# A hand-ordered attention-and-MLP kernel, its instruction order handed to a build-time event model; first loads as token pairs; mask PSUM apart

## Chip, cores, metric

One core of one Trainium2 chip. The metric is the device time of one launch in microseconds (us); lower is better. Names of engines: TensorE (PE in the profile; PEld is its weight load), VectorE (DVE), ScalarE (ACT), GpSimd (POOL), SyncE (SP). SPq, POOLq and ACTq are queues from which transfers are issued.

## The reference

Attention that looks only at the best chunks of keys, then an MLP with a softplus. 4 batches, 8 heads, 768 tokens, head size 64; keys fall into 24 chunks of 32. For each query an upper bound of its score with each chunk is taken from the chunk's minimum and maximum, the 6 chunks with the largest bounds are kept, and softmax runs over those under the causal mask.

```python
k_min, k_max = min and max of k over each chunk of 32 keys
ub = sum over d of max(q * k_min, q * k_max)            # one bound per query and chunk
ub = where(causal, ub, -1e9)
top_chunks = argsort(ub)[..., -6:]
scores = q @ k.T / 8, kept where the chunk is in top_chunks and key <= query
attn = softmax(scores) @ v                               # 4 x 8 x 768 x 64
x = attn, heads side by side                             # 3072 x 512
h = x @ w_in                                             # 512 x 2048
out = softplus(h) @ w_out                                # 2048 x 512
```

## The kernel before

The 3072 tokens are cut into 12 blocks of 256. A block goes through these steps:

1. *prep*: k, q and v are loaded; k and q are turned so that the head size lies on partitions; the chunk extremes `kx`, the bounds `ub` (TensorE), the top 6 (VectorE), and a mask that is turned as well and laid into spare rows of the query tile, so that the score matmul adds it.
2. *scores*: `s_ps` (TensorE), the exponential `pt` (ScalarE), `o_ps` = pt x v (TensorE), division (VectorE), a DMA transpose to `x`.
3. *MLP*: eight groups of eight matmuls `hp` (TensorE), `e_sb` = exp and `g` = ln(1 + e) (ScalarE), then eight groups of four matmuls `y` (TensorE) and the store.

Every engine runs its instructions in the order in which the program lists them. That order was set by hand. Score steps set a slot counter; each slot first runs old work that is due, then some MLP steps by a rate, then whatever an agenda holds for that slot:

```python
def slot(rate):
    cost = 0.0
    for item in list(later):                       # p@v, division, transposes, stores that are due
        if item[0] <= clock[0] and cost < 0.3:
            later.remove(item); cost += item[1]; item[2](*item[3])
    credit[0] += rate
    while credit[0] >= 1.0:                        # MLP steps
        credit[0] -= 1.0
        if next(mlp, "end") == "wait": credit[0] = 0.0
    for g_ in agenda.pop(clock[0], []): next(g_, None)   # prep of later blocks
    ...
    clock[0] += 1

def rate():
    c = clock[0]
    return 0.0 if c < 14 else 1.0 if c < 30 else 0.5 if c < 40 else 1.0 if c < 48 else 0.57 if c < 120 else 1.0
```

The first three blocks are loaded as float32, cast and turned on ScalarE and TensorE, in half blocks; their agenda is a list of numbers (names: c cast, t turn, e evacuate, b extremes, d bounds, `e0` the mask):

```python
stages(f1, ((4, "b0 c0"), (5, "d0"), (6, "ck1 tk1 ek1 cq1 tq1 eq1"), (7, "e0"), (8, "b1 c1"), (9, "d1"), (12, "e1")))
at(11, do(cast_v, 1))
stages(f2, ((18, "ck0 tk0 ck1 ek0"), (19, "b0"), (20, "cq0 tq0 cq1 eq0"), (21, "c0"), (22, "d0"),
            (23, "e0 tk1 ek1"), (24, "b1 tq1 eq1 c1"), (25, "d1"), (27, "e1")))
...
for n in range(3, NB):                             # blocks 3 to 11: loaded as bf16, turned by DMA
    base = 16 * n - 13
    offs = (0, 1, 2, 3, 4, 6, 7, 8, 12)
    turns = (base - 12, max(base - 9, ends[n - 3] + 1))
    if n == 3:
        base, turns = 40, (38, 41)
        offs = (0, 1, 2, 3, 3, 4, 5, 6, 7)
```

The loads of the first blocks take 128 consecutive tokens per transfer, so that one piece is one token of one head, 64 floats or 256 bytes; the mask of a half block uses the one PSUM buffer that the bounds also use:

```python
# load_f32: for t in range(2)
eng[t].dma_start(out=xf[:, t, heads], in_=src[nm][b, heads, r0:r0 + 128].rearrange("h s d -> s h d"))
# prep_first, step e_
mT = ps_t.tile([64, NT, 2, 128], BF16, name="mTh", tag="t")
```

The softmax here doesn't subtract the row's maximum and nothing guards it: scores larger than these inputs give would overflow.

## Time and profile before

| | before |
|---|---|
| time, median of the first 3 runs | 306.91 us (306.29 to 307.59) |
| profiled span | 307.3 us, mean granted TensorE clock 0.972 |
| first hp matmul / first y matmul | 35.97 / 71.05 us |
| first scores of block 3 | 95.18 us |

The page gives each engine's busy time and share of the span, then the span in 40 slices; a digit is the busy share in tenths, and in the row PEclk the clock that TensorE was granted, in tenths (9 is 90% or more). A trace holds clock events only from the first change on, which is at 38.3 us in before; where there is no event, the tools print full clock. The 9s ahead of it are therefore not measured, and the first group of hp matmuls, at 35.97, ran at 1.90 us, the pace of a reduced clock. Of before:

```profile
PE 258.9 (84%) x2472; PEld 182.7 (59%) x2472; DVE 165.2 (54%) x585; ACT 215.8 (70%) x373; POOL 105.7 (34%) x185
...
PE   1545777678768989997989999999999999999984
...
PEclk9999997699969999999999999999999999999999
```

TensorE is the busiest engine, and in the second half it is full. What is left to gain lies in the first 100 to 170 us. The windows view of before, TensorE alone (length, busy time and instructions, granted clock, mean busy DMA share, GB/s):

```profile
core 0: us, PE busy (x), PEclk, DMA share, GB/s
36.00:60.00 24.00, 18.89 (x147) 0.79 0.67 119
60.00:80.00 20.00, 14.80 (x145) 1.00 1.88 155
80.00:100.00 20.00, 14.49 (x105) 0.83 1.14 145
100.00:170.00 70.00, 63.15 (x736) 1.00 1.23 110
170.00:290.00 120.00, 119.22 (x1159) 1.00 0.58 74
```

The clock falls in two of the three windows with holes; 60 to 80, which has as many, stayed at 1.00. The timeline of before shows both (start, length, engine, line, operation, count; in brackets the idle time just before and what ended it). Of the names, `xbk` is the cast k, `kt` and `mt` are the turned keys and the turned mask, `kx` the extremes, and `qa`, `ka` tiles that the score matmul reads:

```profile
39.38 1.04 PE L426 MATMUL hp<-x,w_in_sb 128*128 128x256 bf16 x8
...
44.79 0.40 PE L252 MATMUL xT<-ident,xbk 128*128 128x128 bf16 x4 [1.92 <-ACT xbk L241]
45.02 1.77 PE L426 MATMUL hp<-x,w_in_sb 128*128 128x256 bf16 x8
46.93 1.84 PE L426 MATMUL hp<-x,w_in_sb 128*128 128x256 bf16 x8
...
76.22 3.30 SPq L176 DMA_TRANSPOSE kt<-k_sb  x2
80.64 1.28 DVE L191 TENSOR_REDUCE kx<-kt 128x16 bf16<-128x512 bf16 x2 [1.92 <-DMA kt<-k_sb]
...
91.67 1.20 SPq L339 DMA_TRANSPOSE mt<-mraw  x1
...
95.60 0.98 ACT L366 ACTIVATE pt<-s_ps 128x512 bf16<-128x512 f32 x2 [18.04 <-PE s_ps L364]
```

Two things are to be read here. At 44.79 TensorE waited 1.92 us for a cast (`xbk`) that stood behind other ScalarE work; the next two groups of eight hp matmuls took 1.8 us each, against 1.04 of a group at 39.38. And between 77.6 and 95.6 ScalarE had nothing at all to do for 18 us, since block 3's keys were turned only at 76, its extremes taken at 80.6 and its mask turned at 91.7. TensorE had little but y matmuls in that time, with holes between them, and at a reduced clock: twelve of them took 4.31 us at 89.78, against 2.75 at 78.77.

The waits view of before (who waited, for whom: total us, times, longest):

```profile
ACT pt L366 <- PE s_ps L364: 33.1, 29, 18.0
ACT e_sb L428 <- PE hp L426: 28.7, 53, 1.5
```

### The profile page before, as it was taken

The page shows a single profiled execution, that of the slowest core. Times are in us where ns is not written, and L with a number is a line of the kernel's source. Part 1 is how long each engine was busy: PE and PEld are TensorE (multiplying, and loading weights), DVE is VectorE, ACT ScalarE, POOL GpSimd, SP SyncE. Part 2 cuts the span into 40 slices and gives each one's busy share as a digit, 9 for nine tenths or more (in the row PEclk, how much of TensorE's full clock was granted, in tenths as well). Part 3 has the DMA queues.
Part 4 walks back from the last instruction along what each step waited for, and adds up shares of the span by engine and source line. Part 5 has one row for each costly group of instructions (what it writes and reads, how often), then busy time and mean ns, then how long its engine had stood idle before and what let it go on. Part 6 is the DMA issues. An engine that isn't in the chain of part 4 may idle for free.

```text
span 307.3 us, 6466 instructions
## 1 busy us (share of the span) xinstructions
PE 258.9 (84%) x2472; PEld 182.7 (59%) x2472; DVE 165.2 (54%) x585; ACT 215.8 (70%) x373; POOL 105.7 (34%) x185
## 2 busy tenths in 40 slices
PE   1545777678768989997989999999999999999984
PEld 0323555455325766676667777676777777776631
DVE  6865535331697878975869486783861101210010
ACT  5554597697005897879878888888978879766620
POOL 2554213678413433445574646721111011100000
PEclk9999997699969999999999999999999999999999
DMA  9988390999995897959999999992111011111001
GB/s 167 218 142 171 73 175 17 160 180 126 181 145 121 66 125 102 138 62 136 99 140 123 137 120 146 148 120 69 53 54 51 2 51 36 51 44 43 36 34 68
DMA packets 118082, 31.74 MB, mean 103 GB/s; under 512 B 112420, under 2 KB 114468, under 8 KB 118052
## 3 DMA queue, kind: packets, MB, share of 16 engines
q0 software_dynamic: 58848, 11.28, 53.0%
q1 hardware_dynamic: 57092, 19.54, 32.1%
q10 hardware_dynamic: 2112, 0.52, 1.0%
q8 instruction: 19, 0.31, 0.4%
q14 instruction: 11, 0.09, 0.1%
HBM read 27.26 MB, written 6.29 MB: 109 GB/s over the span
## 4 chain that ended last, share of the span: by engine, by line
PE 64%; ACT 16%; DVE 10%; issue 5%; DMA 4%; SPq 0%; POOL 0%; ACTq 0%
PE hp L426 22%; PE y L442 22%; PE s_ps L362 6%; PE o_ps L387 5%; ACT pt L366 5%; ACT e_sb L428 4%; PE s_ps L364 4%; ACT g L430 4%; DVE kx L191 2%; PE xT L252 1%; DMA kt<-k_sb 1%; DVE y_sb L447 1%; DMA mt<-mraw 1%; DMA two<-in_q_dram 1%; ACT xbq L241 1%
## 5 line engine op out<-in xcount | busy, mean ns | idle before, releaser
L366 ACT ACTIVATE pt<-s_ps 128x512 bf16<-128x512 f32 (+1 forms) x192 | 97.4, 539 | 35.2 <-PE s_ps L364 33.1
L426 PE MATMUL hp<-x,w_in_sb 128*128 128x256 bf16 x768 | 103.8, 280 | 0.2 <-ACT e_sb L428 0.2
L442 PE MATMUL y<-w_out_sb,g 128*128 128x512 bf16 x384 | 99.3, 386 | 5.2 <-DVE y_sb L447 5.2
L370 POOL TENSOR_SCALAR_AFFINE_SELECT pt<-pt 128x256 bf16<-128x256 bf16 x96 | 40.0, 419 | 139.5 <-ACT pt L366 136.9
L426 PEld LDWEIGHTS <-w_in_sb 128*128 128x128 bf16 x768 | 73.8, 100 | 12.5 <-issue 0.3
L428 ACT ACTIVATE e_sb<-hp 128x512 f32<-128x512 f32 x96 | 57.3, 597 | 29.6 <-PE hp L426 28.7
L442 PEld LDWEIGHTS <-g 128*128 128x128 bf16 x384 | 35.3, 98 | 34.7 <-issue 9.0
L430 ACT ACTIVATE g<-e_sb 128x1024 bf16<-128x1024 f32 x48 | 50.7, 1057 | 1.5
L447 DVE COPY y_sb<-y 128x512 f32<-128x512 f32 x24 | 16.6, 690 | 47.5 <-PE y L442 47.5
L393 DVE RECIPROCAL rec<-o_ps 128x4 f32<-128x4 f32 x48 | 8.5, 177 | 55.0 <-PE o_ps L387 54.9
L362 PE MATMUL s_ps<-qa,ka 96*128 96x256 bf16 x96 | 26.7, 282 | 8.9 <-ACT pt L366 5.3
L387 PE MATMUL o_ps<-v,pt 128*128 128x65 bf16 x672 | 31.7, 196 | 0.0
L362 PE MATMUL s_ps<-qt,kb 128*128 128x256 bf16 x96 | 26.9, 281 | 4.2 <-ACT pt L366 3.8
L387 PEld LDWEIGHTS <-pt 128*128 128x128 bf16 x672 | 28.7, 99 | 2.0 <-issue 0.2
L364 PE MATMUL s_ps<-qt,kb 128*128 128x256 bf16 (+1 forms) x96 | 24.1, 252 | 0.0
L191 DVE TENSOR_REDUCE kx<-kt 128x16 bf16<-128x512 bf16 x36 | 22.8, 676 | 2.0 <-DMA kt<-k_sb 1.9
L364 PE MATMUL s_ps<-qa,ka 96*128 96x256 bf16 (+1 forms) x96 | 23.9, 252 | 0.0
L397 DVE TENSOR_TENSOR o_sb<-o_ps,rec 128x256 bf16<-128x256 f32 x48 | 20.4, 425 | 1.7
L116 POOL DMA_DIRECT2D k_sb<-in_k_dram x18 | 16.5, 918 | 3.7 <-DMA kt<-k_sb 3.1
L116 POOL DMA_DIRECT2D q_sb<-in_q_dram x18 | 16.3, 906 | 1.5 <-issue 1.0
L364 PEld LDWEIGHTS <-ka 96*128 96x128 bf16 x96 | 9.5, 99 | 12.1 <-issue 9.2
L110 POOL DMA_DIRECT2D v<-in_v_dram x18 | 16.1, 897 | 0.7 <-issue 0.3
(68 smaller groups left out, 226.2 us busy)
## 6 DMA issues: line engine op xcount, KB each, us to landing
out_dram<-y_sb SPq DMA_DIRECT2D x24, 256.0 KB, 2.3
k_sb<-in_k_dram POOLq DMA_DIRECT2D x18, 128.0 KB, 5.2
q_sb<-in_q_dram POOLq DMA_DIRECT2D x18, 128.0 KB, 5.1
v<-in_v_dram POOLq DMA_DIRECT2D x18, 128.0 KB, 5.1
w_in_sb<-in_moe_w_in_dram POOLq DMA_DIRECT2D x4, 512.0 KB, 8.0
w_out_sb<-in_moe_w_out_dram POOLq DMA_DIRECT2D x4, 512.0 KB, 8.8
two<-in_v_dram SPq DMA_DIRECT2D x6, 256.0 KB, 5.0
two<-in_k_dram SPq DMA_DIRECT2D x4, 256.0 KB, 4.6
```

The source lines that it names most:

```text
L116: nc.gpsimd.dma_start(out=xb[:, t], in_=rows(nm, n, t))
L191: nc.vector.tensor_reduce(kx[:, :, m].rearrange("d p t c -> d t p c"), kT.rearrange("d t p (c e) -> d t p c e", e=CH), axis=AX.X, op=op)
L362: nc.tensor.matmul(s_ps[:, 0:QB], kk[0:nr, p, j * 128:(j + 1) * 128], qq[0:nr, :, p, :], start=True, stop=True)
L364: nc.tensor.matmul(s_ps[:, QB:w], kk[0:nr, p, (j + 1) * 128:(j + 2) * 128], qq[0:nr, 1 if last else 0:, p, :], start=True, stop=True)
L366: nc.scalar.activation(pt[:, h, j:j + 2].rearrange("k j c -> k (j c)")[:, 0:w], s_ps[:, 0:w], ACT.Exp, scale=scale)
L370: nc.gpsimd.affine_select(out=diag, in_=diag, compare_op=ALU.is_ge, fill=0.0, base=0, channel_multiplier=-1, pattern=[[0, 2], [1, 128]])
L387: nc.tensor.matmul(o_ps[:, u, h], pt[:, h, j, c0:c0 + 128], V[b % 2][:, j, 2 * p + h, :], start=(j == 0), stop=(j == t0 + u))
L397: nc.vector.tensor_tensor(o_sb[:, :, p % 2], o_ps[:, :, :, 0:D], rec.to_broadcast([128, NT, 2, D]), op=ALU.mult)
L426: nc.tensor.matmul(hp[:, fi], w_in_sb[:, dt, ft * 128:(ft + 1) * 128], X[n][:, dt // 2, :, dt % 2, :], start=(dt == 0), stop=(dt == KDM - 1))
L428: nc.scalar.activation(e_sb[:, f2 * 2:f2 * 2 + 2], hp, ACT.Exp)
L430: nc.scalar.activation(g[:, f4 * 4:(f4 + 1) * 4], e_sb, ACT.Ln, bias=1.0)
L442: nc.tensor.matmul(y, g[:, f, u * 128:(u + 1) * 128], w_out_sb[:, f, :], start=(f == 0), stop=(f == KFF - 1))
```

## The change

The intent: instead of agenda numbers, every instruction group becomes an `Op` with an engine, a duration, dependencies, the buffers that it takes and gives back, and a target time as its key. At build time a small event simulation runs all five engines; when an engine comes free, it takes the op with the lowest key among those whose inputs are there and whose buffers are free (or waits a little if a more urgent one is about to be ready). The order so found is the program's order. The arithmetic stays. Core of the diff (cut; some lines folded):

```diff
-later, slot, rate, agenda, IDLE, stages, run_block ...      # all hand-set order goes
+LEAD0, LEAD, SLACK = 26.0, 42.0, 0.3
+LAT = {"PE": 0.25, "ACT": 0.14, "DVE": 0.12, "POOL": 0.12, "SP": 0.1}
+class Op: eng, dur, fn, key, deps, take, drop, dma
+def run_plan():
+    while left:
+        t = heapq.heappop(times)
+        for e, lst in ready.items():
+            if free[e] > t: continue
+            for o in lst:
+                if o.avail <= t and (pick is None or o.key < pick.key) and room(o): pick = o
+            ...
+            o.start = t; free[e] = t + o.dur
+            if o.dma is None: o.done = t + o.dur + LAT[e]
+            else:                                   # transfers: one server per ring
+                service, lat, ring = o.dma
+                begin = max(t + o.dur + 0.8, dma_free.get(ring, 0.0))
+                dma_free[ring] = begin + service
+                o.done = begin + service + lat
+            o.fn()                                  # here the instruction is written
+for n in range(NB):                                 # targets: VM for the MLP, VA for prep and scores
+    VM[n] = t_; t_ += 14.0 + 2.4 * (blocks[n][1] + 1)
+    VA[n] = 8.0 * n if n < 3 else VM[n] - LEAD
+so = op("PE", 0.17 if last else 0.222, f_s, key, ...)        # scores
+ho = op("PE", 0.87, f_h, VM[n] + i * step, ...)              # eight hp matmuls
+xo = op("ACT", 0.55, f_x, ...)                               # e_sb
+yo = op("PE", 0.87, f_y, VM[n + 1] + ..., ...)               # four y matmuls
```

Two parts are not order. The k and q loads of the first three blocks take token pairs, 512 bytes a piece and half as many pieces; the ScalarE copies that take the turned tiles out of PSUM undo the interleave by writing every second element. And the half-block mask takes a buffer of the `o_ps` pool instead of the one that the bounds use:

```diff
-eng[t].dma_start(out=xf[:, t, heads], in_=rows(nm, n, t, ...))                 # t = 0, 1
+eng.dma_start(out=dst, in_=src[nm][b, h0:h1, block].rearrange("h (s t) d -> s h (t d)", t=2))
-nc.scalar.copy(kth, xT)
+nc.scalar.copy(kt.rearrange("d p (s t) -> d t p s", t=2), xT)
-mT = ps_t.tile([64, NT, 2, 128], BF16, name="mTh", tag="t")
+mT = Buf("ps_o")
```

`w_in` is requested earlier (when k of block 1 has landed, not when q has), `w_out` too, v of blocks 0 and 1 goes into buffers of its own, and six memsets move from VectorE to GpSimd. The hp matmuls had not waited for `w_in` before: it had landed by 29.35, and the first hp came at 35.97.

## The prediction

> **What bounds it now.** The span is 307.3 us and TensorE is the limit, unevenly. I priced its work from warm groups of the timeline: eight hp matmuls 0.87 us, four y 0.87, a score matmul 0.11 (256 columns) or 0.06 (128), o_ps 0.031, a bound 0.03. With the counts of the table of groups that is about 240 us, an estimate; some 67 us are lost. Counts per window show where: 26 before the first hp at 36.0; 11 in 35-60; 6 in 60-80; 8 in 80-100; 8 in 100-170; almost nothing in 170-290 (PE busy 97-100%); 6 at the end.
>
> The holes have three causes in the timeline and waits. (1) ScalarE's program order at 44-66: prep of block 2 is wedged between MLP steps. (2) Block 3: ScalarE idles 18.0 us before the pt at 95.6, behind the kt transposes at 76, kx, bounds, mask transposes. (3) Cold TensorE: granted clock 0.66-0.85 in 40-60 and 80-100; eight hp matmuls took 1.7-1.9 us there. "TensorE: Matmul & The Clock Gate" (Trainium skill, Part 1) says that idling halves the clock and sustained work restores it; the trace agrees, about 8 us lost (estimate).
>
> **What changes.** Arithmetic is the same; PE has the same number of rows, ACT 11 fewer, DVE 6 fewer. k and q loads of the first three blocks become 512-byte pieces instead of 256, which "DMA: Bandwidth & Descriptors" (Specifications) names as the minimum for full rate; copies now undo the interleave by strided writes. kx reads SBUF, not PSUM: 676 against 686 ns, neutral. Memsets move to POOL. The mask transpose uses an o_ps buffer, so the next half's bounds don't wait behind it in the single ps_t.
>
> Order matters more. Nearly all prep of blocks 0-2 comes before the first MLP step; y of block 0 starts after four hp groups; block 3's k, q, v are requested right after w_out; block 3's scores come after 21 hp groups and 11 y groups.
>
> **Critical path.** ScalarE has about 29 us of ramp work ordered before its first e_sb (12 casts of 0.62, 11 copies of 0.59, 6 v casts, 5 mask copies, 16 exps): starting near 4, it can't take an hp before 33-34 (before: 37.9). Gain about 4. From there to block 3's scores ScalarE has about 32 us and TensorE 34: dense, so warm. Those scores should start at 68-75 instead of 95, with about three groups more of MLP done: another 20-24 us. In 100-170 perhaps 2 of 8 us return, since blocks of 768 keys load ScalarE (about 22 us each) as much as TensorE; the end is unchanged; some 2 us of new stalls where real DMA times exceed the model's.
>
> 307 - 4 - 22 - 2 + 2 = 281. **Predicted 281 us, 80% range 271 to 293.** Chances: faster by over 2% 0.94, within 2% 0.04, slower 0.02.
>
> **What would show it.** First e_sb at 32-36; no casts after 45; PE busy over 85% of 40-100; granted clock near 1.0 after 40; the longest wait of pt for s_ps under 5; block 3's scores before 76; ScalarE busy 75-80%, TensorE 90% or more.
>
> **What would make it wrong.** w_out late (8.8 us median to landing), so that y, early in the in-order queue, blocks hp; kt or mt transposes (4-5 us) queued on SP behind others; a model optimistic by some tenths per step, turning steady state from no loss to 5%; score-heavy stretches leaving TensorE waiting for exps. If block 3 still starts after 85, expect 290 or more.

## The result and the profile after

| | before | after |
|---|---|---|
| time, median of 4 runs | 307.25 us (306.29 to 309.02) | 284.73 us (284.25 to 286.96) |
| profiled span | 307.3 us | 283.3 us |
| mean granted TensorE clock | 0.972 | 0.997 |
| first hp / first e_sb | 35.97 / 37.90 us | 37.82 / 42.17 us |
| first y | 71.05 us | 45.84 us |
| first scores of block 3 | 95.18 us | 80.94 us |

The ratio is 0.9275, with a 95% interval from 0.9209 to 0.9341. A ratio here is the mean time of one kernel's fast runs over the mean of the other's fast runs of the same rounds, so it is not quite the ratio of the medians in the table. Executions over 1.5% slower than the fastest of the same kernel are left out of the means. The outputs are correct. The profiled execution of before was the slowest of its four (309.02 us), so the spans differ by 24.0 us and the medians by 22.5.

The page after:

```profile
PE 246.8 (87%) x2436; PEld 181.7 (64%) x2472; DVE 165.5 (58%) x579; ACT 213.5 (75%) x373; POOL 107.4 (38%) x191
...
PE   1372689888999999998999999999999999998974
...
PEclk9999999999999999999999999999999999999998
```

The weight loads (PEld) are 2472 in both, so the matmul work is the same; 36 matmul records are missing after (all of y: 348 of 384), so 87% is too low. The variant a_winlate below, which runs the same instructions and whose trace has all 2472, shows 250.9 us and 90%. The windows of TensorE after:

```profile
core 0: us, PE busy (x), PEclk, DMA share, GB/s
38.00:60.00 22.00, 18.62 (x210) 1.00 1.79 174
60.00:80.00 20.00, 17.96 (x149) 1.00 1.95 146
80.00:100.00 20.00, 18.85 (x188) 1.00 1.11 130
100.00:170.00 70.00, 67.23 (x754) 1.00 1.41 135
170.00:260.00 90.00, 88.48 (x884) 1.00 0.18 50
```

No window has a reduced clock (the events of this trace begin at 39.0 and show full clock until 281), and the stretch from 38 to 100 is dense. In the timeline after, `vf` is v as it was loaded:

```profile
5.03 6.28 SPq L338 DMA_DIRECT2D vf<-in_v_dram  x4
8.95 2.44 POOL L360 DMA_DIRECT2D w_in_sb<-in_moe_w_in_dram  x4
24.21 1.38 ACT L216 CAST v<-vf 128x512 bf16<-128x512 f32 x2 [4.20 <-DMA vf<-in_v_dram]
...
37.82 1.63 PE L690 MATMUL hp<-x,w_in_sb 128*128 128x256 bf16 x8
39.45 1.04 PE L690 MATMUL hp<-x,w_in_sb 128*128 128x256 bf16 x8
42.17 1.09 ACT L698 ACTIVATE e_sb<-hp 128x512 f32<-128x512 f32 x2
...
55.19 1.25 SPq L503 DMA_TRANSPOSE kt<-k_sb  x1
62.96 0.42 DVE L557 COPY ka<-kt 64x1024 bf16<-64x1024 bf16 x1 [3.52 <-DMA kt<-k_sb]
72.11 1.19 SPq L552 DMA_TRANSPOSE mt<-mraw  x1
73.96 0.42 DVE L557 COPY ka<-kt 64x1024 bf16<-64x1024 bf16 x1 [1.88 <-DMA kt<-k_sb]
78.98 0.73 DVE L567 COPY qa<-mt 32x512 bf16<-32x512 bf16 x1
80.94 0.27 PE L611 MATMUL s_ps<-qa,ka 96*128 96x256 bf16 x1
```

The first three lines are a new wait: v of blocks 0 and 1 was issued from 5.0 on, that of block 1 at 8.55 and 10.27, `w_in` from another queue at 8.95, and ScalarE stood 4.2 us until v of block 1 had landed, 15.6 us after its issue. The lines from 55 on are block 3: its keys are turned 21 us earlier than before, but that transpose took 7.75 us to land, and the mask copy at 78.98 stands in VectorE's order behind block 4's keys, for which VectorE waited at 73.96. TensorE had no idle time just before the score at 80.94: it came from MLP work. The waits after:

```profile
ACT e_sb L698 <- PE hp L690: 22.8, 31, 3.6
ACT pt L620 <- PE s_ps L613: 18.0, 42, 1.4
...
ACT v L216 <- DMA vf<-in_v_dram: 4.2, 1, 4.2
```

The 18 us wait of `pt` is gone; the longest is 1.4 us.

**Where the time came from.** I priced TensorE's work from warm groups (eight hp 0.87 us, four y 0.87, a first score matmul 0.11, a second 0.083 on average, o_ps 0.031, a bound 0.03, a turn 0.09 to 0.1; an estimate from the traces) and counted weight loads, of which no record is missing, in each window. The window's length less that work is what TensorE lost there:

| window | lost before | lost after | difference |
|---|---|---|---|
| 0 to 38 us | 27.8 | 27.4 | -0.4 |
| 38 to 100 | 24.7 | 8.1 | -16.6 |
| 100 to 170 | 8.8 | 2.5 | -6.3 |
| 170 to the end | 7.6 | 6.7 | -0.9 |
| sum | 68.9 | 44.7 | -24.2 |

The difference is the difference of the spans, 24.0 us, within the rounding; so the gain is lost time of TensorE that is no longer lost, two thirds of it between 38 and 100 us.

### The profile page after: what moved, and what is told of

Read it like the earlier page. It is cut to its first block, busy times and chain, and to the rows that moved or that the text cites. A ratio compares the mean times of both kernels' runs of the same rounds, so it can differ in the third digit from the quotient of the medians.

```text
span 283.3 us, 6429 instructions
## 1 busy us (share of the span) xinstructions
PE 246.8 (87%) x2436; PEld 181.7 (64%) x2472; DVE 165.5 (58%) x579; ACT 213.5 (75%) x373; POOL 107.4 (38%) x191
## 4 chain that ended last, share of the span: by engine, by line
PE 61%; DMA 16%; DVE 11%; SPq 4%; ACT 3%; issue 2%; POOL 1%; POOLq 0%; ACTq 0%
PE y L711 23%; PE hp L690 21%; DMA kt<-k_sb 8%; PE s_ps L611 6%; PE o_ps L640 5%; DMA vf<-in_v_dram 5%; PE s_ps L613 4%; DMA qt<-q_sb 3%; DVE kx L283 2%; SPq L338 2%; DVE y_sb L719 2%; ACT pt L620 1%; SPq L278 1%; DVE o_sb L655 1%; DVE qt L568 1%
## 5 line engine op out<-in xcount | busy, mean ns | idle before, releaser
L690 PE MATMUL hp<-x,w_in_sb 128*128 128x256 bf16 x768 | 98.6, 274 | 0.0
L711 PE MATMUL y<-w_out_sb,g 128*128 128x512 bf16 x348 | 91.9, 379 | 5.9 <-DVE y_sb L719 3.9
L640 PEld LDWEIGHTS <-pt 128*128 128x128 bf16 x672 | 27.1, 99 | 9.3 <-POOL pt L627 5.7
L611 PE MATMUL s_ps<-qt,kb 128*128 128x256 bf16 x96 | 25.7, 280 | 5.7 <-ACT pt L620 5.7
L611 PE MATMUL s_ps<-qa,ka 96*128 96x256 bf16 x96 | 25.7, 284 | 2.5 <-DVE qa L468 1.9
L613 PE MATMUL s_ps<-qt,kb 128*128 128x256 bf16 (+1 forms) x96 | 23.1, 251 | 0.0
L613 PE MATMUL s_ps<-qa,ka 96*128 96x256 bf16 (+1 forms) x96 | 23.0, 252 | 0.0
L497 POOL DMA_DIRECT2D k_sb<-in_k_dram x18 | 16.2, 901 | 16.8 <-DMA kt<-k_sb 16.6
L613 PEld LDWEIGHTS <-kb 128*128 128x128 bf16 x96 | 9.5, 99 | 9.5 <-issue 6.3
```

What stands on the lines that cost most here:

```text
L497: nc.gpsimd.dma_start(out=xb[nm].tile[:, t], in_=rows(nm, n, t))
L611: nc.tensor.matmul(s_ps[:, 0:QB], kk[0:nr, p, j * 128:(j + 1) * 128], qq[0:nr, :, p, :], start=True, stop=True)
L613: nc.tensor.matmul(s_ps[:, QB:w], kk[0:nr, p, (j + 1) * 128:(j + 2) * 128], qq[0:nr, 1 if last else 0:, p, :], start=True, stop=True)
L640: nc.tensor.matmul(ob.tile[:, u, h], ptb.tile[:, h, j, c0:c0 + 128], V[b % 2][:, j, 2 * p + h, :], start=(j == 0), stop=(j == t0 + u))
L690: nc.tensor.matmul(hp[:, fi], w_in_sb[:, dt, ft * 128:(ft + 1) * 128], xb.tile[:, dt // 2, :, dt % 2, :], start=(dt == 0), stop=(dt == KDM ...
L711: nc.tensor.matmul(y, gb.tile[:, f, u * 128:(u + 1) * 128], w_out_sb[:, f, :], start=(f == 0), stop=(f == KFF - 1))
```

## The experiments

Twelve runs were made, in three groups: b_parts, a_ref, a_plain and a_mask_t; then a_ref2, a_vlate, a_winlate and a_unif; then a_fix_t, a_pert, best1 and a_lead3. Each group shared its chip and its runs of before, and the ratios are all to before on that chip. In the first group, theory 1 was that the order alone makes the gain; theory 2 that the loads and the mask buffer carry a good part of it. Later groups follow up on the wait for v and on the plan itself.

### a_ref: the changed kernel again

No edit.

> The changed kernel once more, unaltered, as the yardstick of this call. Both theories expect its recorded ratio to the kernel before, 0.927 within the interval 0.921 to 0.934, so about 285 us, with the first hp matmul near 38 and the first scores of block 3 near 81.

Measured: 286.34 us (284.11 to 289.29, the last slow), ratio 0.9287 [0.9251, 0.9323]. The result repeats. The profiled execution had a span of 285.4, 2.1 us more than the one shown above, with the same program. Its timeline says where:

```profile
39.86 1.73 PE L690 MATMUL hp<-x,w_in_sb 128*128 128x256 bf16 x8
44.72 1.89 PE L690 MATMUL hp<-x,w_in_sb 128*128 128x256 bf16 x8
47.14 1.51 PE L690 MATMUL hp<-x,w_in_sb 128*128 128x256 bf16 x8
```

Its windows view, TensorE alone, says at what clock the last two ran:

```profile
44.80:48.00 3.20, 3.20 (x17) 0.50 1.28 204
```

Three further groups ran cold (at a reduced clock) where the other execution was warm from 39.45. The Trainium skill, page "TensorE: Matmul & The Clock Gate", Part 1, says that the activity window that decides the clock is free-running, so that the moment of the change depends on where the first matmul falls in it. These two traces agree: in both, the clock events after the first one lie multiples of 3.41 us apart, but the grid lies differently. One execution had the full clock from 39.0 on; the other rose at 41.3, fell to half from 44.7 to 48.1 after a hole of 2.0 us, and was full from then on. The spans differ by 2.1 us. The six recorded times fit it roughly: 284.11 to 286.24 us at a mean clock of 0.997 to 0.999, 286.44 to 289.29 at 0.991 and 0.992.

### b_parts: the old order with token pairs and the mask apart

```diff
-eng[t].dma_start(out=xf[:, t, ...], in_=rows(nm, n, t, ...))
+e_.dma_start(out=pairs(xf)[:, hs]..., in_=....rearrange("h (s t) d -> s h (t d)", t=2))
-nc.scalar.copy(H2["k", g][1], xT)
+nc.scalar.copy(kp.rearrange("d p (s t) -> d t p s", t=2), xT)
-mT = ps_t.tile([64, NT, 2, 128], BF16, name="mTh", tag="t")
+mT = ps_o.tile([64, NT, 2, 128], BF16, name="mTh", tag="o")
```

> The kernel before with the two small parts of the change (k and q of the first three blocks loaded as token pairs, mask transpose into an o_ps buffer; kx read from SBUF because pairs need it) and its old order of instructions. Theory 1, the order makes the gain: 304 to 309 us, no verdict of faster. Theory 2, the faster loads and the freed PSUM buffer make a good part of it: 296 to 302 us, with the first hp matmul 3 us or more earlier than 36.

Measured: 307.62 us, ratio 0.9999 [0.9969, 1.0029]. First hp at 36.60 (before 35.97), block 3's scores at 93.33, losses 9.6, 5.4 and 7.3 us in 38–60, 60–80 and 80–100 (before 9.9, 6.0, 8.8). Under the old order the two parts have no measurable worth. The SP queue was done with the first loads at 10.7 us instead of 13.3, but nothing had waited for them: the waits view of neither kernel has a cast of v that waits. Their copies even cost more: 0.73 us against 0.585 for the same 128x512 tile.

### a_plain: the new order with 256-byte loads

```diff
-eng_of[eng].dma_start(out=dst, in_=rows2(nm, n, h0, h1))
+for t in range(2):
+    eng_of[eng].dma_start(out=two[n].tile[:, "kq".index(nm), h0:h1, t], in_=rows(nm, n, t, h0, h1))
-copy(EK[n], kt.rearrange("d p (s t) -> d t p s", t=2), xT["k"].tile)     # and the same for q
+copy(EK[n], kt.rearrange("d p (t s) -> d t p s", t=2), xT["k"].tile)
```

> The changed kernel with k and q of the first three blocks loaded in 256-byte pieces again (two DMAs per tensor instead of one, plain copies out of PSUM), planned anew. Theory 1: 283 to 287 us; the copies of xT get back from 0.73 to 0.59 us (12 of them, 1.8 us of ScalarE) and the DMA issues on the SP queue take twice as long, which about cancels. Theory 2: 290 us or more and a first cast over 1 us later.

Measured: 292.20 us (291.65 to 294.25), ratio 0.9508 [0.9469, 0.9548], about 6.8 us slower than a_ref (0.0221 of 307.94). Theory 1 had 283 to 287 and missed; theory 2's 290 or more came true, but not its sign, a first cast over 1 us later (5.01 us here against 4.66 in the trace of after). This kernel was planned anew, so the 6.8 us are those of the loads and of another plan together. First hp at 42.03 (37.83 in a_ref), losses 14.1 and 9.1 us in 20–38 and 38–60 (12.3 and 6.6). The timeline of a_plain shows what happened to v:

```profile
8.75 12.96 SPq L338 DMA_DIRECT2D vf<-in_v_dram  x4
...
25.23 0.62 ACT L216 CAST v<-vf 128x512 bf16<-128x512 f32 x1 [6.10 <-DMA vf<-in_v_dram]
```

The v loads are the same four transfers as in the changed kernel. But the k and q loads ahead of them are twice as many, and kept the SP queue until 8.7 us instead of 4.8 in a_ref: the first four issues took 2.09 us, the first two with pairs 1.00, so about 0.5 us each, and a pair transfer of 256 KB landed in a median of 4.1 us, no longer than one of 128 KB without pairs. v therefore went out from 8.75 instead of 4.88 and met `w_in` (from 10.38 on) with three of its four loads: the one issued at 8.75 landed after 4.93 us, the others after 14.8 to 15.3. In a_ref only the two of block 1 took so long (15.8 and 14.8), those of block 0 6.7 and 6.1. So here ScalarE waited 6.1 us for v of block 0, and TensorE's o_ps, for the cast of that v, 5.7 us of the same time. The first hp, 4.2 us later, goes back to this as far as one trace shows; the rest of the 6.8 us is not taken apart from the new plan. And the pairs halve both the transfers and the pieces ahead of v; no run tells which of the two counts. The page "Perfetto Trace Analysis" ("What 'DMA-bound' means") says of an issuing queue whose track is solid with slices that this is descriptor generation, not data movement, and that large descriptors are what matter. The trace agrees that SP's track is solid, from 0.81 to 21.7 us; the 12.96 us are three issues of 1.14 us and one of 9.39, and how much of them is generation and how much waiting no run here tells apart.

### a_mask_t and a_fix_t: the mask's buffer

a_mask_t plans the mask with the old pool:

```diff
-mT = Buf("ps_o")
+mT = Buf("ps_t")
```

> The changed kernel with the mask transpose back in the single ps_t buffer, planned anew. Theory 1: within 2 us of the changed kernel (284 to 287), since only twelve mask transposes of blocks 0 to 2 are concerned. Theory 2: 288 us or more, lost before 60 us where the bounds of one half then wait for the mask copies of the other.

Measured: 282.05 us (281.28 to 282.63), ratio 0.9161 [0.9136, 0.9187]: 4 us *faster* than the changed kernel. Neither theory had that. Since the plan looks at buffers, this one-word edit changes both the buffer and, through the plan, the order of everything behind it. So a_fix_t keeps the changed kernel's order on every engine and changes only the tile that is used:

```diff
-mt = make(mT, [64, NT, 2, 128], BF16, "mTh")
+mt = mT.tile = pools["ps_t"].tile([64, NT, 2, 128], BF16, name="mTh", tag="ps_t")
```

> The changed kernel in exactly its own order of instructions on every engine (compared: the same), with the mask transpose's tile in the single ps_t buffer instead of an o_ps buffer. Theory P, the o_ps buffers are the worse place, since masks and attention outputs then wait for each other: about 282, as with the planned version a_mask_t. Theory S, the 4 us of a_mask_t came from another plan and not from the buffer: 284 to 289, as the changed kernel.

Measured: 286.67 us (284.65 to 288.50), ratio 0.9303 [0.9263, 0.9342], the same as the changed kernel (0.9287 and, below, 0.9306). So the buffer by itself does nothing measurable in this order; the 4 us of a_mask_t are those of another plan. This pair is worth remembering: in a planned kernel a small edit is not a small edit of the order.

### a_ref2: the changed kernel, on the second group's chip

No edit.

> The changed kernel unaltered, as the yardstick of this call: 0.927 of the kernel before.

Measured: median 287.30 us, ratio of the fast runs 0.9306 [0.9269, 0.9343]. One of its six executions, the profiled one, took 528.2 us. From the groups of that trace (line, engine, operation, count; busy us, mean ns):

```profile
L711 PE MATMUL y<-w_out_sb,g 128*128 128x512 bf16 x384 | 197.5, 678 | 2.3 <-DVE y_sb L719 2.3
L690 PE MATMUL hp<-x,w_in_sb 128*128 128x256 bf16 x768 | 196.9, 444 | 0.0
```

A y matmul took 678 ns on average instead of 379, an hp matmul 444 instead of 274. From start to start, an hp matmul took 222 ns at the median against 109 and a y matmul 444 against 216: TensorE ran at half speed for the whole execution, while exponentials kept their time (`pt` 542 ns against 543). This trace holds no clock event at all, and the 1.00 in its result is what the tools print then. The same page on the clock gate warns, under "HAM trace caveats" ("Seeing it yourself"), that such records can be unreliable and the clock can be stuck low; it speaks of a quarter for 50 us and more, here it was a half for the whole 526.5 us span.

### a_vlate and a_winlate: the wait for v

After the result, theory A was that the ramp lost its predicted 4 us to ScalarE's wait for v of block 1. a_vlate tells the model a later landing of that v, so that the plan casts it later; nothing of the transfers changes:

```diff
-[buf] if t == 0 else [], [], (1.3, 1.5, "load"))
+[buf] if t == 0 else [], [], (1.3, 12.0 if n == 1 else 1.5, "load"))
```

> The changed kernel with one number of its model put right: the v loads of block 1 are said to land 12 us after their turn instead of 1.5 (the trace shows 14.7 us from issue to landing, behind w_in). The planner then puts block 0's last exps before the v casts. Theory A, the ScalarE wait of 4.2 us for these loads is what ate the expected gain of the ramp: the wait is gone, block 0's second half of scores comes 3 to 4 us earlier, the first hp matmul at 33.5 to 35.5 instead of 37.8, total 280 to 283. Theory B, the wait is slack because the x transposes and block 2's loads (held behind w_in) decide: the wait is gone but the first hp stays at 36.5 or later and the total within 1 us of the changed kernel.

a_winlate lets v land undisturbed: `w_in` is held until v of block 1 is there instead of k of block 1.

```diff
-hold1 = op("POOL", 0.2, ... tensor_copy(gate, two[1].tile[0:1, 0, 7, 1, 0:1]), -9, [ld["k", 1]])
+hold1 = op("POOL", 0.2, ... tensor_copy(gate, vbuf[1].tile[0:1, 1, 7, 0:1]), -9, [ld["v", 1, 1]], [], [vbuf[1]])
```

> The changed kernel with the w_in load held back until the last v of block 1 has landed, instead of k of block 1. Theory A, contention with w_in delays v: v of block 1 lands by 15 to 17 instead of 25 and ScalarE does not wait for it, but k and q of block 2 (gated behind w_in) come 4 to 6 us later; first hp at 34 to 37, total 281 to 286. Theory B, the v loads are slow of themselves: v lands after 20 still, ScalarE still waits.

Measured: a_vlate 284.45 us (283.45 to 285.47), ratio 0.9236 [0.9212, 0.9259]. The wait is down to 0.2 us and the first hp comes at 33.52, 4.3 us earlier, as theory A had it. But the time is only 2.2 us better than a_ref2 (0.9306 less 0.9236 of 308), where theory A had 280 to 283. The first e_sb came at 40.40 and block 3's scores at 80.56, both hardly earlier, and 60–80 lost 3.8 us instead of 1.8 in a_ref. Here the earlier start came back as holes in the next stages; between 66.0 and 69.4 the clock was at half again.

a_winlate: 281.22 us (280.66 to 281.83), ratio 0.9131 [0.9110, 0.9153], the lowest ratio (those of a_lead3 and a_mask_t overlap with it): 0.981 of the changed kernel on the same chip (0.9131 / 0.9306). Its timeline:

```profile
15.18 0.18 POOL L360 COPY gate<-vf 1x1 f32<-1x1 f32 x1 [0.67 <-DMA vf<-in_v_dram]
15.31 2.29 POOL L362 DMA_DIRECT2D w_in_sb<-in_moe_w_in_dram  x4
19.72 1.17 ACT L216 CAST v<-vf 128x512 bf16<-128x512 f32 x2
...
35.72 1.91 PE L692 MATMUL hp<-x,w_in_sb 128*128 128x256 bf16 x8
```

v is there at 15.2 and its cast starts at 19.72 without a wait. The two v loads of block 1 landed 5.65 and 4.83 us after their issue; in after, where `w_in` ran beside them from the GpSimd queue, it took 15.6 and 14.7 (medians of all four v loads: 6.1 against 10.7). The page "DMA: Bandwidth & Descriptors", "Issuing engines are not separate DMA queues", says that DMAs of several engines interleave on the same 16 DMA engines, and that a second issuing engine saves only the issue time, "usually small relative to the DMA itself". The first half agrees with these landings. The second holds only loosely here: without `w_in` beside them, each v load took 1.0 to 1.9 us to issue against 4.8 to 7.0 to land. Four in a row took 6.45 us, so the last of them waited longer for its turn in the queue (5.4 us) than it then took to land. So theory A is right that the wait was caused by `w_in`. That removing it is what made this kernel faster is not shown, because the plan changed as well: a_winlate loses 3.1 us in 38–60 where a_vlate, also without the wait, loses 5.8 (with half clock from 42.1 to 45.5); and a_mask_t and a_lead3, which keep the wait (4.3 and 4.1 us), are as fast (0.9161 and 0.9152).

### best1: both faster edits together

The edits of a_winlate and a_mask_t in one kernel.

> Both alterations that gained alone: w_in held back until v of block 1 has landed, and the mask transpose planned in ps_t. If the gains were separate causes they add: 277 to 279 us. If a_mask_t was only a better draw of plan: 279 to 284, no better than a_winlate's 281.

Measured: 285.02 us (283.92 to 288.11), ratio 0.9276 [0.9230, 0.9322], worse than either alone (0.9131 and 0.9161) and above both expectations. It lost 4.3 us in 60–80, a_winlate 1.4. These two gains did not add up.

### a_unif and a_pert: what the durations are worth

a_unif gives every op the mean duration of its engine; dependencies, buffers, keys and the transfer model stay:

```diff
+for e in LAT:
+    same = [o for o in ops if o.eng == e]
+    mean = sum(o.dur for o in same) / len(same)
+    for o in same: o.dur = mean
```

> The changed kernel with every operation of an engine given that engine's mean duration in the model; keys, dependencies, buffers and DMA times are as they were. If the durations matter to the order: 291 us or more, lost in waits of TensorE for exps and for hp buffers between 40 and 170. If the keys (the targets of each block) and the dependencies make the order: within 3 us of the changed kernel, 282 to 288.

Measured: 300.82 us (300.48 to 301.79), ratio 0.9772 [0.9748, 0.9796]. So about 14 us of the 22 went with the durations that tell a 0.17 us score from a 0.87 us group, more than planned kernels scatter (a_pert); 7 us come even without. Block 3's scores were at 91.37 and 100–120 lost 10.1 us (0.8 after), partly at a reduced clock again. Of its windows:

```profile
100.00:120.00 20.00, 14.95 (x162) 0.83 1.93 146
```

a_pert multiplies every duration by a random factor between 0.95 and 1.05:

```diff
-o = Op(eng, dur, fn, key, ...)
+o = Op(eng, dur * rnd.uniform(0.95, 1.05), fn, key, ...)
```

> The changed kernel with every duration of its model multiplied by a random factor between 0.95 and 1.05, everything else the same: how far plans that are equally informed scatter. Theory S (plans scatter by several us): 280 to 290, differing from the changed kernel's 286 by 1 us or more in either direction. Theory P: within 1 us of 286.

Measured: 288.96 us (287.50 to 289.79), ratio 0.9368 [0.9332, 0.9404], with 4.5 us lost in 140–170 (0.3 after). This one draw of errors up to 5% came out about 0.7% slower than a_fix_t (same chip and the changed kernel's order; the intervals just overlap), small against the gain; what such errors cost in general one draw can't say. With a_mask_t, best1, a_lead3 and a_vlate it shows how planned kernels of the same instructions scatter: their medians lie between 281 and 289 us.

### a_lead3: is block 3 held by its target time?

Block 3's prep and scores get a target 8 us later.

```diff
-VA[n] = 8.0 * n if n < RAMP else VM[n] - LEAD
+VA[n] = 8.0 * n if n < RAMP else VM[n] - LEAD + (8.0 if n == 3 else 0.0)
```

> The changed kernel with the target time of block 3 moved 8 us later (so its k, q, v are wanted and its prep planned later). If the early request of block 3 is what brings its scores forward, as the prediction had it: first scores of block 3 at 85 to 89 instead of 81, total 287 to 292. If the SP queue and the transposes decide (kt issued at 55, behind the x transposes, landing at 63): scores stay within 2 us of 81 and the total within 3 us of 286.

Measured: 281.83 us (280.63 to 283.30), ratio 0.9152 [0.9119, 0.9185]. Block 3's scores came at 81.52, against 80.94 and 82.46 in the two traces of the changed kernel: the target does not set them. Its keys were turned at 56.16 (55.19 and 57.47). The total was expected within 3 us of 286 or above it, and is 4 us lower: another plan again. In all planned kernels but a_plain and a_unif block 3's scores lie between 79.8 and 83, whatever else changes. What sets them is not shown. The chain seen in the timeline of after (the transposes on the SP queue, 7.75 us for block 3's keys and 8.02 for block 4's, and the mask copy behind block 4's keys on VectorE) is a lower limit: that copy ended at 79.71. But the landing of block 3's keys alone does not decide, since it took 4.73 us in a_lead3 and the scores came no earlier; and TensorE did not wait for the chain. In after and in every other planned trace of a fast run it went from MLP groups to these scores without idle time, and by the plan's order 19 to 22 hp and 11 to 13 y groups stood ahead of them (24 and 16 in a_unif). No experiment took either away.

## Why the prediction was right, and where it was off

It said 281 us (271 to 293), faster; measured 284.73. Its mechanism stands: the loss lay in the holes and cold stretches before 100 us, and a denser order took them away. Its sum, term by term (the measured values are the differences of lost time in the table above):

| term | predicted | measured | |
|---|---|---|---|
| ramp, "Gain about 4" | -4 | -0.4 | mis-sized |
| middle, "another 20-24 us" | -22 | -16.6 | mis-sized |
| 100–170, "perhaps 2 of 8 us return" | -2 | -6.3 | mis-sized, the other way |
| the end, and "some 2 us of new stalls" | +2 | -0.9 | not separable |
| sum | -26 | -24.2 | |

So the total is close partly because misses of opposite sign met, which is luck. The rows are windows of time: new stalls can't be told apart in them, and the one that was found, 4.2 us for v, lies in the first row.

- **The ramp.** The step that failed: "ScalarE has about 29 us of ramp work ordered before its first e_sb ...: starting near 4, it can't take an hp before 33-34". As a lower limit it is true; as an estimate it left out the transfers. ScalarE waited 4.2 us for v, and it had exponentials and block 2's copies ahead of the first e_sb. e_sb came at 42.17, not in 32 to 36, and hp 1.9 us later than before. a_vlate and a_winlate took the wait away; only a_vlate then had hp in the predicted range (33.52), with little total gain.
- **Block 3.** Predicted at 68 to 75, "before 76"; it came at 80.94. When it came, 20 hp groups and 12 y groups had been issued (by weight loads; before: 16 and 12), so 14.2 us earlier and four groups, 3.5 us, more of MLP. The prediction named the danger itself ("kt or mt transposes (4-5 us) queued on SP behind others"), and the landings of 7.75 and 8.02 us were worse than the 4–5 it took from before; but TensorE did not wait for these scores (a_lead3), so how much of the 6 us is due to that stays open. The delay as such cost little: a_ref lost 1.8 us in 60–80.
- **After 100 us.** The hand order lost 8.8 us there and the plan 2.5, so the plan is better in the mixed stretch too; the prediction thought that ScalarE limits that stretch. a_unif's 10.1 us in 100–120 and a_pert's 4.5 in 140–170 show that this stretch depends on how well the plan fits.
- **The pairs.** The prediction counted the loads as neutral to helpful in landing time. Without them, and planned anew, the kernel is 6.8 us slower: more transfers stand ahead of v in the SP queue (a_plain), which it did not see. How much of the 6.8 us is the other plan is open. The mask buffer, of which it expected that bounds no longer wait, has no measurable worth (a_fix_t).
- **The clock.** Predicted "near 1.0 after 40": right (1.00 in every window from 38 to 260). How much of the gain is clock alone was not tested apart. The events bound it: before stood at half clock for 17.1 us between 45.2 and 93.0, after for none until 281, so the slower clock by itself can make at most half of that, 8.5 of the 24 us (an estimate from these events).

Its signs, one by one: no casts after 45 (last v cast at 41.08): right. PE busy over 85% of 40–100: right as a whole (18.62 of 22, 17.96 of 20 and 18.85 of 20 from 38 to 100, or 89%, with records missing). Longest wait of pt under 5: right (1.4). ScalarE busy 75–80%: 75%, right. TensorE 90% or more: not decided, 87% with 36 records missing, and 89 and 90% in the complete traces of a_vlate and a_winlate, which are other plans. First e_sb and block 3's scores: wrong, as said. Its count of 11 fewer ScalarE instructions is not in the profile (373 in both); VectorE's 6 fewer are.

What stays open: why one plan is 281 us and another 289 (no single wait explains it; only that order matters and small edits reshuffle it), and how much of a_winlate's gain is the plan's luck.

## What to carry to other kernels

When a hand-set order leaves the limiting engine holes early on, an order from a simple event model with measured durations can close most of them; what it can't plan for is what it has wrong, here transfers that slow each other down and the time that the issuing queue itself takes. Such waits are "<- DMA" in the new trace; but taking the largest one away was worth only 2.2 us in a_vlate. An edit whose worth depends on the order must be tested inside the new order: the pairs were worth nothing before, and leaving them out after, with a new plan, cost 6.8 us. And to test one edit of a planned kernel, freeze the order (as a_fix_t did); otherwise a reshuffle of some 1–2% is measured together with it.

## What the Trainium skill lacked or had wrong

- Page "DMA: Bandwidth & Descriptors", "Issuing engines are not separate DMA queues": issue time is called usually small relative to the DMA. Here a 256 KB load of 256-byte pieces took 1.0 to 1.9 us to issue from the SP queue and 4.8 to 7.0 us to land (a_winlate, without `w_in` beside it), so issue is not small once several stand in a row: four took 6.45 us, and 12.96 us in a_plain, 9.39 of it one issue. I found no figure there of what an issue costs when the queue is busy.
- The same page gives a bandwidth for DMA transposes, but nothing that I found on their landing under load: `kt<-k_sb` landed in 3.1 to 8.0 us within one execution (median 4.8).
- Page "TensorE: Matmul & The Clock Gate", "HAM trace caveats": its example of a stuck clock is a quarter for 50 us and more. One of the runs here was at half speed for all of its 526.5 us (y matmuls 444 ns apart against 216), with no clock event in the trace. I found no word there that a trace may hold no event ahead of the first change, as here up to 38 to 46 us.
- Page "SBUF — State Buffer" (the note on cachelines in "Door 1: The DMA port swizzle") lets one stride up to 8 bf16 elements for free. ScalarE's copy out of PSUM that writes every second bf16 took 0.73 us against 0.585 for the same 128x512 tile written without a stride (b_parts and before; a_ref and a_plain alike).
